# A kernel of linear attention and a gated feed-forward layer: own products of late blocks in halves of 64 keys, past products per head, in two phases over two PSUM banks

## The chip, the cores and the metric

One Trainium2 chip, one of its cores. The metric is the device time of one execution in microseconds, the median of three runs. A NeuronCore has a matrix engine (TensorE, PE in the profile, its weight loads PEld), a vector engine (DVE), a scalar engine (ACT), GpSimd (POOL), and SyncE (SP), which issues most DMAs here. Each works through its own list of instructions in order, and they wait for each other on semaphores. TensorE writes to PSUM, which has 8 banks of 2 KB in each of 128 partitions.

## The reference

`r`, `k`, `v`, `w` have the shape (4, 8, 768, 48): batch, heads, tokens, head dimension. Per head a 48 × 48 state runs over the tokens; its output goes through a feed-forward layer from 384 to 2048 and back.

```python
for t in range(S):
    kt, vt, rt, wt = (k[:, :, t], v[:, :, t], r[:, :, t], w[:, :, t])
    cur = np.einsum('bhd,bhe->bhde', u[None] * kt, vt)
    y[:, :, t] = np.einsum('bhd,bhde->bhe', rt, state + cur)
    state = wt[:, :, :, None] * state + np.einsum('bhd,bhe->bhde', kt, vt)
...
x = attn_out.transpose(0, 2, 1, 3).reshape(B * S, H * D)
h = x @ w_in
g = h * np.cos(h)
return g @ w_out
```

## The kernel before

**Chunks and blocks.** The tokens are cut in 24 chunks of 128 (six for each of four sequences). Two chunks make a block `i`, 12 blocks in all. Blocks 0 and 1 hold the first chunks of the four sequences, which have no past. A chunk holds eight heads as four pairs `p` with two heads `h` each; head `h` of a pair lies in partitions 64h to 64h + 47 (`rows(h)`).

**What a chunk needs.** VectorE makes products of the decays and scales `r` and `k` by them. `att_scores` makes k·r (`pa`); `placed` puts the allowed half of them into `asb`, on whose diagonal GpSimd has put the bonus terms (`picked`). `asb[h][:, p]` is a matrix of 128 keys by 128 queries of which the part above the diagonal counts. For chunks from 6 on (`ALL_OF`), the pairs 2 and 3 (`TURNED`) have the two halves of 64 keys and of 64 queries in swapped order, and `in_order` swaps the queries back as it reads. The output `y` of a chunk is the sum of two kinds of products:
- own products (`att_own`): `v` by `asb`, the keys of the chunk itself;
- past products (`att_past`): the state before the chunk (`past`) by the scaled `r`.

Both write to `py`, two banks of three groups of 128 columns for the two chunks of a block. The 48 output rows of a head lie as 32 rows in the group kt = 0 or 2 (`LONG`, eight places for a chunk) and 16 rows in the group kt = 1, where two heads share 32 rows (`middle`). Before the change an own product has 128 keys by 32 columns of `v` for 128 queries, 16 for a chunk; a past product has 48 rows for the places of `LONG` (L490) and 112 rows, both heads together, for the four middles (L486). `att_state` then makes the chunk's contribution to the state (`pst`, L423), in all blocks but the last two.

**The feed-forward layer.** ScalarE casts `py` to `xT` (`high`), VectorE makes the rest that the cast lost (`low`). A block has eight slots; `mm1` of a slot makes `ph` from `xT` and the weights (18 products of 256 columns, L571), `gate` runs over four engines (steps I, S, N, M, H, L), and `mm2`, two slots later, adds 12 products of 384 columns to `acc` (L589).

**The order.** It is written by hand: the string `START` for the slots of blocks 0 and 1, then for each slot a row of `PLAN`, whose tokens name a step and a chunk or block. A block's own products, past products and state sums are the tokens `o`, `p`, `s` in row 6 of the block before:

```python
"o+1 p+1 s+1 mm1 load+7 lv+6 lv+7 X+1 n+1 I S c+4 N M mm2 H L d+4",
```

For block 2 they stand near the end of `START` (`o2 L13 p2 mm2.12 mm2.13 I15 ... s2`). `load` and `lv` are DMAs of SP, `X` makes `xT`, `n` adds up the state, `c` ends with the next pick of `asb`, `d` places the next `past`. PSUM banks of the kind "a" are taken in turn by `bank`; from block 2 on there are four of them (`BANKS`, stage 3), used by `pa`, `pt`, `py` and `pst`.

Of the kernel before, what the change touches and what calls it, by code (L numbers as in the profile page):

```python
# [10 lines left out]
F32 = mybir.dt.float32  # L11
# [11 lines left out]
C = 128  # L23
HD = 48
NP = 4
R96 = 2 * HD
ROW = 64
# [3 lines left out]
BLK = 2  # L31
# [11 lines left out]
BANKS = dict(a=("a0", "a1", "a2", "acc0", "acc1"), h=("h0", "h1", "h2")), dict(a=("a0", "a1"), h=("h0", "h1")), dict(a=("a0", "a1", "a2"), h=("h0", "h1", "h2")), dict(a=("a0", "a1", "a2", "h2"), h=("h0", "h1"))  # L43
PAIR_W = 2 * HD + 16
VW = NP * PAIR_W
TURNED = 2
ALL_OF = 6
# [44 lines left out]
             o="a lv", s="t d lv", p="o d")  # L92
# [3 lines left out]
def rwkv_cos_ffn(ctx: ExitStack, tc: tile.TileContext, tr, tn, tv, u, ut, wts, w, rkw, vst, us, xs, out):  # L96
    nc = tc.nc
# [5 lines left out]
    FU = 512 // BT  # L103
    wts = wts.bitcast(I16)

    cst = ctx.enter_context(tc.tile_pool(name="cst", bufs=1))
# [3 lines left out]
    ps = fast.enter_context(tc.tile_pool(name="ps", bufs=1, space=bass.MemoryType.PSUM))  # L110
    turn = {"a": 0, "h": 0}
# [26 lines left out]
    wholes = cst.tile([R, NG, NP], F32, name="wholes")  # L138
    wmax = cst.tile([128, 1], F32, name="wmax")
    nc.vector.memset(wmax, 0.0)  # L140
    ones = cst.tile([128, 1], F32, name="ones")
    nc.vector.memset(ones, 1.0)
    past = [cst.tile([R, NP, R96], F32, name="past%d" % n) for n in range(BLK)]
# [293 lines left out]
    def v_col(p, h):  # L437

        return p * PAIR_W + h * (HD + 16)

    def att_own(i):

        py = [bank("a", [128, 3, C], "py") for half in range(2)]

        def at(kt, n, q):

            side, col = divmod(kt * BLK + n, 3)
            return py[side][32 * q:32 * q + 32, col]

        outs[i] = py, at  # L450
        for step, n in enumerate(sorted(range(BLK), key=lambda n: placed_at.get(i * BLK + n, n))):
            a = atts[i * BLK + n]

            def long_ones(sides, heads):
                for kt, p, h, q in LONG:
                    if kt in sides and h in heads:
                        col = v_col(p, h) + 16 * h
                        nc.tensor.matmul(out=at(kt, n, q), lhsT=a["v"][:, col:col + 32], rhs=in_order(a, a["asb", h][:, p], p),  # L458
                                         start=step == 0, stop=a["c"] == 0, skip_group_check=True)

            def middle(h):
                for p in range(NP):
                    col = p * PAIR_W + (48 if h else 32)
                    nc.tensor.matmul(out=at(1, n, p), lhsT=a["v"][:, col:col + 32], rhs=in_order(a, a["asb", h][:, p], p),  # L464
                                     start=False, stop=a["c"] == 0, skip_group_check=True)

            if step == 0:
                long_ones((0, 2), (0, 1))
                middle(0)
                middle(1)  # L470
            else:
                alone = 0 if n == BLK - 1 else 2
                long_ones((0, 2), (0,))
                middle(0)
                long_ones((alone,), (1,))
                long_ones((2 - alone,), (1,))
                middle(1)

    def att_past(i):

        py, at = outs.pop(i)
        two = [atts[i * BLK + n] for n in range(BLK)]
        if two[0]["c"] > 0:
            for n, a in enumerate(two):
                for p in range(NP):
                    nc.tensor.matmul(out=at(1, n, p), lhsT=a["past"][:, p, 32:64], rhs=in_order(a, a["r3"][:, p], p),  # L486
                                     start=False, stop=True, skip_group_check=True)
            for n, a in enumerate(two):
# [12 lines left out]
        def low(side):  # L501
            low_part("x", halves_of["x"][:, 1, side], py[side].rearrange("p k t -> p (k t)"), halves_of["x"][:, 0, side])

        def less(side):
            nc.tensor.matmul(out=py[side].rearrange("p k t -> p (k t)"), lhsT=nident, rhs=halves_of["x"][:, 0, side], start=False, stop=True, skip_group_check=True)

        def taken(side):
            nc.scalar.copy(out=halves_of["x"][:, 1, side], in_=py[side].rearrange("p k t -> p (k t)"))
# [50 lines left out]
    def mm1(t, half=None):  # L559
        i, u = seq[t]  # L560
        if not half:
            for j in range(BLK):
                att(i * BLK + j, "x")
            units[t] = bank("h", [C, FU, BT], "ph")
        xT, ph = xts[i], units[t]
        for fi in range(FU) if half is None else (half,):
            steps_of = [(kt, a, b) for kt in range(KT) for a, b in PASSES]
            if half is not None:
                steps_of.sort(key=lambda x: (x[1], x[2]))
            for n, (kt, a, b) in enumerate(steps_of):  # L570
# [240 lines left out]
    return [b * NCB + c for c in range(NCB) for b in range(n // NCB)]  # L811


def x_pieces():

    for kt, p, h, q in LONG:
        yield p, h, 16 * h, kt, 32 * q, 32
    for h in range(2):
        for p in range(NP):
            yield p, h, 0 if h else 32, 1, 32 * p + 16 * h, 16  # L820


def one_by_one(tc, rkw, vst, us, xs, out, ident, halves, wgt, gate):
# [147 lines left out]
```

## Time and profile before

| | |
|---|---|
| median of three runs | 507.66 us (507.04 to 508.62) |
| the profiled execution's own time | 509.25 us |
| its span, first to last instruction | 507.5 us |
| busy: PE, PEld | 501.5 us, 487.5 us |
| busy: DVE, ACT, POOL | 378.9, 256.0, 202.5 us |
| granted TensorE clock, mean | 0.992 of 2.4 GHz |

The page and the views behind it show one profiled execution. Busy is the time in which at least one instruction of an engine ran; products on TensorE overlap, so a row of a timeline gives the start of its first record and the time to the end of its last. "[0.20 <-X]" at a row's end is the idle time of the engine before it and what ended it. An fp32 product of the program stands as two records in the trace, an fp32r product (L571, L589) as one.

### The profile page before, as it was taken

What the parts mean: (1) busy time and instruction counts of PE and PEld (TensorE: products, weight loads), DVE (VectorE), ACT (ScalarE), POOL (GpSimd) and SP (SyncE); (2) the same over time, 40 slices, a digit from 0 to 9 for tenths busy, and PEclk for the clock granted to TensorE, in tenths of its full rate; (3) what the DMA queues carried; (4) which work ended last, traced back from release to release, by engine and by line L of the source; (5) the groups of instructions that cost most, each with busy time, mean ns of one, the idle gap of its engine ahead of it and who ended that gap; (6) DMA issues with size and microseconds to landing.
All of it is one profiled execution on the core that took longest, in us unless ns stands there. A gap on an engine that the chain in (4) does not pass through costs nothing.

```text
span 507.5 us, 12744 instructions
## 1 busy us (share of the span) xinstructions
PE 501.5 (99%) x5334; PEld 487.5 (96%) x5334; DVE 378.9 (75%) x669; ACT 256.0 (50%) x440; POOL 202.5 (40%) x273
## 2 busy tenths in 40 slices
PE   8999999999999999999999999999999999999997
PEld 8899999999999999999999999999999999999997
DVE  7989999777969758848947946956966975587633
ACT  2769788525355444444445435435444544544543
POOL 3434546435445335334333524523533533423330
PEclk9979999999999999999999999999999999999999
DMA  8978550142052051051040132113105103013001
GB/s 270 416 292 286 228 227 2 63 162 96 34 193 63 1 193 63 1 194 52 13 172 36 51 113 83 63 53 141 63 4 192 62 3 125 33 56 132 32 3 34
DMA packets 17324, 54.59 MB, mean 108 GB/s; under 512 B 2032, under 2 KB 8688, under 8 KB 17264
## 3 DMA queue, kind: packets, MB, share of 16 engines
q1 hardware_dynamic: 17120, 53.64, 29.7%
q8 instruction: 43, 0.70, 0.6%
q14 instruction: 17, 0.14, 0.1%
q10 hardware_dynamic: 144, 0.10, 0.1%
HBM read 49.02 MB, written 4.72 MB: 106 GB/s over the span
## 4 chain that ended last, share of the span: by engine, by line
PE 95%; DMA 2%; SPq 1%; ACT 0%; issue 0%; DVE 0%; DVEq 0%; ACTq 0%
PE ph L571 41%; PE acc L589 40%; PE pa L378 3%; DMA raw<-wts 2%; PE py L458 2%; PE py L464 2%; PE pst L423 2%; PE pt L401 2%; PE py L490 1%; PE py L486 1%; PE pa L370 1%; PE pc L307 1%; SPq L244 1%; SPq L262 0%; SPq L177 0%
## 5 line engine op out<-in xcount | busy, mean ns | idle before, releaser
L171 POOL TENSOR_TENSOR gs<-rr,gs 128x256 fp32r<-128x256 f32 x188 | 148.6, 811 | 236.9 <-ACT gs L168 214.2
L571 PE MATMUL ph<-xT,w 128*128 128x256 f32 x1728 | 222.2, 283 | 0.2 <-DVE w L202 0.2
L571 PEld LDWEIGHTS ph<-xT,w 128*128 128x128 f32 x1728 | 214.2, 190 | 2.3 <-PE py L490 0.4
L589 PE MATMUL acc<-w,gs 128*128 128x384 f32 x1152 | 215.6, 337 | 0.0
L589 PEld LDWEIGHTS acc<-w,gs 128*128 128x128 f32 x1152 | 196.1, 188 | 0.3 <-issue 0.2
L537 DVE SCALAR_TENSOR_TENSOR rr<-rr,ph 128x512 f32<-128x512 int32 x96 | 65.5, 682 | 63.6 <-ACT rr L534 62.5
L550 ACT ACTIVATE rr<-rr,quarter 128x512 f32<-128x512 f32 x96 | 69.5, 724 | 79.9 <-DVE rr L537 79.7
L534 ACT ACTIVATE rr<-ph 128x512 int32<-128x512 f32 x96 | 57.3, 597 | 68.3 <-PE ph L571 67.8
L168 ACT CAST gs<-rr 128x512 fp32r<-128x512 f32 x88 | 54.6, 621 | 63.2 <-DVE rr L551 39.1
L551 DVE TENSOR_TENSOR rr<-rr,ph 128x512 f32<-128x512 f32 x96 | 65.5, 682 | 22.3 <-ACT rr L550 20.0
L331 POOL TENSOR_SCALAR_AFFINE_SELECT asb<-cd 128x512 f32<-128x512 f32 x48 | 40.8, 876 | 53.2 <-DVE cd L321 35.5
L392 DVE COPY_PREDICATED asb<-turned_mask,pa 64x128 f32<-64x128 uint8 (+1 forms) x108 | 33.6, 346 | 2.1 <-POOL asb L331 0.3
L279 DVE TENSOR_TENSOR_SCAN ee<-tt,one_e 112x516 f32<-112x516 f32 (+1 forms) x25 | 31.6, 1269 | 2.0 <-DMA tt<-tr 2.0
L285 DVE TENSOR_TENSOR_SCAN tt<-tt,inj 112x516 f32<-112x516 f32 x24 | 30.3, 1262 | 0.8
L171 DVE TENSOR_TENSOR xT<-py,xT 128x384 fp32r<-128x384 f32 x22 | 11.3, 551 | 21.4 <-ACT xT L168 21.4
L192 ACT ACTIVATE top<-raw 128x768 f16<-128x768 bf16 x16 | 17.5, 1091 | 2.7 <-DMA raw<-wts 2.7
L458 PE MATMUL py<-asb,v 128*32 128x128 f32 x384 | 17.4, 276 | 0.0
L200 DVE CUSTOM_DVE_ANT_0 h<-h,top 128x1536 uint16<-128x1536 uint16 x16 | 16.1, 1005 | 1.7 <-ACT top L192 0.9
L464 PE MATMUL py<-asb,v 128*32 128x128 f32 x384 | 17.1, 273 | 0.0
L168 ACT CAST xT<-py 128x384 fp32r<-128x384 f32 x24 | 10.3, 482 | 12.7 <-PE py L490 11.6
L168 ACT COPY past<-dd 48x192 f32<-48x192 f32 x40 | 14.0, 349 | 2.7 <-DVE dd L354 2.4
L378 PEld LDWEIGHTS pa<-tt 48*64 48x64 f32 x576 | 12.9, 133 | 2.2 <-issue 2.2
(89 smaller groups left out, 364.4 us busy)
## 6 DMA issues: line engine op xcount, KB each, us to landing
tt<-tr SPq DMA_DIRECT2D x22, 770.5 KB, 6.6
raw<-wts SPq DMA_DIRECT2D x16, 767.8 KB, 6.9
rk<-tn SPq DMA_DIRECT2D x18, 384.0 KB, 3.2
v<-tv SPq DMA_DIRECT2D x24, 224.0 KB, 4.7
ww<-w SPq DMA_DIRECT2D x6, 768.0 KB, 5.1
out<-ob SPq DMA_DIRECT2D x23, 192.0 KB, 2.0
tt<-tr SPq DMA_DIRECT2D x4, 256.0 KB, 4.0
tt<-tr SPq DMA_DIRECT2D x1, 258.5 KB, 4.3
```

Of the source, the lines that this page charges most:

```text
L168: (nc.scalar.copy if E[name] is nc.scalar else E[name].tensor_copy)(out=out, in_=in_)
L171: E[name].tensor_tensor(out=out, in0=full, in1=high.bitcast(F32), op=ALU.subtract)
L279: nc.vector.tensor_tensor_scan(out=ee[:, pairs].rearrange("p a t -> p (a t)")[:, ::-1], data0=wp[:, cols][:, ::-1], data1=one_e[:, pairs]. ...
L285: nc.vector.tensor_tensor_scan(out=wp[:, 0:W129], data0=wp[:, 0:W129], data1=inj.rearrange("p a t -> p (a t)"), initial=0.0, op0=ALU.mult, ...
L331: nc.gpsimd.affine_select(out=asb, in_=col.unsqueeze(2).to_broadcast([C, NP, C]), pattern=[[0, 4], [1, C]], compare_op=ALU.is_equal, fill= ...
L392: nc.vector.copy_predicated(*(which(x) for x in (a["asb", h], turned_mask, pa[h])))
L534: nc.scalar.activation(made["rr"].bitcast(I32), ph, AF.Copy, scale=INV2PI / W_SCALE, bias=0.25)
L537: nc.vector.scalar_tensor_tensor(out=made["rr"], in0=made["rr"].bitcast(I32), scalar=-2.0 * math.pi * W_SCALE, in1=ph, op0=ALU.mult, op1=A ...
L550: N=lambda: nc.scalar.activation(made["rr"], made["rr"], AF.Sin, scale=1.0 / W_SCALE, bias=quarter),
L551: M=lambda: nc.vector.tensor_tensor(out=made["rr"], in0=made["rr"], in1=ph, op=ALU.mult), H=high, L=low)
L571: nc.tensor.matmul(out=ph[:, fi], lhsT=wgt[u * FU + fi][:, 0, a, kt * 128:(kt + 1) * 128], rhs=xT[:, b, kt], start=n == 0, stop=n == 3 * K ...
L589: nc.tensor.matmul(out=accs[i][j][:, :DM], lhsT=gs[:, a, fi, j * C:(j + 1) * C], rhs=wgt[u * FU + fi][:, 1, b], start=u == 0 and fi == 0 a ...
```

## The change

For blocks 3 to 11, `att_own` now only takes the two banks. `att_past` makes the products in two phases. Own products are cut in two halves of 64 keys each, of which the half that is earlier in time is multiplied for all 128 queries and the later one for its last 64 queries only (the quarter left out is masked). Past products are all 48 rows by 32 columns, the middles too, one for each head. In a phase the products in the lower 64 rows of the array write to one bank and those in the upper 64 rows to the other; the second phase swaps the banks. Between the phases stand a product of one column (`apart`) into a bank of its own, the state sums, and a second `apart`. Each bank of `py` now holds its three groups as kt = 0, 1, 2, and kt = 2 holds the other chunk: so `ph` reads `xT` for kt = 2 in two halves of 128 tokens in swapped order, and the casts write three pieces. The middles of the second heads move by two places (`middle_at`). In block 2 the own products stay at full height; the past products stand in two phases around them, and a ScalarE copy (`seen_past`) reads what the first phase wrote before the own products write there.

```diff
+    def apart(tag):
+
+        nc.tensor.matmul(out=ps.tile([C, 512], F32, tag=tag, name="apart")[:32, :1], lhsT=ident[:ROW, :32], rhs=ident[:ROW, :1], start=True, stop=True)
+
+    def past_products(i, at, phase, begins):
+
+        two = [atts[i * BLK + n] for n in range(BLK)]
+        ends = [(kt, phase ^ h ^ kt // 2, p, h, q, 64 * h) for kt, p, h, q in LONG]
+        middles = [(1, phase ^ h, p, h, middle_at(p, h), 32) for h in range(2) for p in range(NP)]
+        for kt, n, p, h, q, col in ends + middles:
+            a = two[n]
+            nc.tensor.matmul(out=at(kt, n, q), lhsT=a["past"][rows(h), p, col:col + 32], rhs=in_order(a, a["r3"][rows(h), p], p),
+                             start=begins and kt != 1, stop=True, skip_group_check=True)
+
+    def own_products(i, at, phase):
+
+        two = [atts[i * BLK + n] for n in range(BLK)]
+
+        def half(lower, kt, p, h, q, whole):
+            n = phase ^ lower ^ kt // 2
+            a = two[n]
+            keys = slice(ROW, C) if lower else slice(0, ROW)
+            col = p * PAIR_W + (48 if h else 32) if kt == 1 else v_col(p, h) + 16 * h
+            x = a["asb", h][keys, p]
+            out, x = (at(kt, n, q), in_order(a, x, p)) if whole else (at(kt, n, q)[:, ROW:], x[:, keys])
+            nc.tensor.matmul(out=out, lhsT=a["v"][keys, col:col + 32], rhs=x,
+                             start=phase == 0 and whole and kt != 1, stop=False, skip_group_check=True)
+
+        for places in LONG, [(1, p, h, middle_at(p, h)) for h in range(2) for p in range(NP)]:
+            for whole in (True, False):
+                for lower in range(2):
+                    for kt, p, h, q in places:
+                        if (lower == (p >= TURNED)) == whole:
+                            half(lower, kt, p, h, q, whole)
+
     def att_own(i):
...
-            side, col = divmod(kt * BLK + n, 3)
-            return py[side][32 * q:32 * q + 32, col]
+            return py[n ^ kt // 2][32 * q:32 * q + 32, kt]
 
         outs[i] = py, at
+        if i * BLK >= ALL_OF:
+            return
+        old = atts[i * BLK]["c"] > 0
+        if old:
+            past_products(i, at, 0, True)
+            nc.scalar.copy(out=seen_past, in_=at(1, 1, NP - 1)[:, :1])
...
+        if old:
+            past_products(i, at, 1, False)
 
     def att_past(i):
 
         py, at = outs.pop(i)
-        two = [atts[i * BLK + n] for n in range(BLK)]
-        if two[0]["c"] > 0:
-            for n, a in enumerate(two):
-                for p in range(NP):
-                    nc.tensor.matmul(out=at(1, n, p), lhsT=a["past"][:, p, 32:64], rhs=in_order(a, a["r3"][:, p], p),
-                                     start=False, stop=True, skip_group_check=True)
-            for n, a in enumerate(two):
-                for kt, p, h, q in LONG:
-                    nc.tensor.matmul(out=at(kt, n, q), lhsT=a["past"][rows(h), p, 64 * h:64 * h + 32],
-                                     rhs=in_order(a, a["r3"][rows(h), p], p), start=False, stop=True, skip_group_check=True)
+        if i * BLK >= ALL_OF:
+            for phase in range(2):
+                own_products(i, at, phase)
+                past_products(i, at, phase, False)
+                if phase == 0:
+                    turn["a"] += 1
+                    tag = BANKS[stage[0]]["a"][turn["a"] % len(BANKS[stage[0]]["a"])]
+                    apart(tag)
+                    att(i, "s")
+                    apart(tag)
...
-            halves_of["x"] = xts[i].rearrange("p o k t -> p o (k t)").rearrange("p o (s n) -> p o s n", s=2)
-            copy("xh", halves_of["x"][:, 0, side], py[side].rearrange("p k t -> p (k t)"))
+            halves_of["x"] = xts[i].rearrange("p o k (s t) -> p o s k t", s=2)
+            copy("xh", halves_of["x"][:, 0, side], py[side])
...
-                nc.tensor.matmul(out=ph[:, fi], lhsT=wgt[u * FU + fi][:, 0, a, kt * 128:(kt + 1) * 128], rhs=xT[:, b, kt],
+                tokens = xT[:, b, kt] if kt < 2 else xT[:, b, kt].rearrange("p (n t) -> p n t", n=BLK)[:, ::-1]
+                nc.tensor.matmul(out=ph[:, fi], lhsT=wgt[u * FU + fi][:, 0, a, kt * 128:(kt + 1) * 128], rhs=tokens,
...
+def middle_at(p, h):
+
+    return (p + NP // 2 * h) % NP
```

How the instructions stand, first for a late block (block 3) on TensorE. A row has the line, the operation, output and inputs, the output's size (partitions by columns) and how many such follow each other. Before, own products, past products and state sums in a row:

```order
L458 MATMUL py<-asb,v 32x128 x8
L464 MATMUL py<-asb,v 32x128 x8
L458 MATMUL py<-asb,v 32x128 x4
L464 MATMUL py<-asb,v 32x128 x4
L458 MATMUL py<-asb,v 32x128 x4
L464 MATMUL py<-asb,v 32x128 x4
L486 MATMUL py<-tt,past_89 32x128 x4
L486 MATMUL py<-tt,past_90 32x128 x4
L490 MATMUL py<-tt,past_89 32x128 x8
L490 MATMUL py<-tt,past_90 32x128 x8
L423 MATMUL pst<-v,kn 64x48
L423 MATMUL pst<-v,kn 48x48
```

The same place of the changed kernel, the first phase up to the state sums (L467 is `own_products`, L453 `past_products`, L444 `apart`, L424 `att_state`):

```order
L467 MATMUL py<-asb,v 32x128 x8
L467 MATMUL py<-asb,v 32x64 x8
L467 MATMUL py<-asb,v 32x128 x8
L467 MATMUL py<-asb,v 32x64 x8
L453 MATMUL py<-tt,past_90 32x128 x2
L453 MATMUL py<-tt,past_91 32x128 x4
L453 MATMUL py<-tt,past_90 32x128 x6
L453 MATMUL py<-tt,past_91 32x128 x4
L444 MATMUL apart<-ident 32x1
L424 MATMUL pst<-v,kn 64x48
L424 MATMUL pst<-v,kn 48x48
```

After 16 state sums a second `apart` and the second phase with the same counts follow, then `ph`; so the state sums now stand inside the products of `py`, and 56 products have become 96. In blocks 10 and 11, which have no state sums, the two `apart` stand next to each other.

The second place is block 2 on TensorE in the changed kernel, from the end of a slot's `ph` to the next `acc` (L499 and L505 are what L458 and L464 were):

```order
L614 MATMUL ph<-xT,w_1206 128x256 x9
L453 MATMUL py<-tt,past_90 32x128 x2
L453 MATMUL py<-tt,past_91 32x128 x4
L453 MATMUL py<-tt,past_90 32x128 x6
L453 MATMUL py<-tt,past_91 32x128 x4
L499 MATMUL py<-asb,v 32x128 x8
L505 MATMUL py<-asb,v 32x128 x8
```

Before, the own products stood directly behind that `ph`, and the past products behind them. The rest of the own products follows, and then the past products of the second phase. On ScalarE the copy that TensorE waits for between them stands here, ahead of the next slot's first step of the gate (L576):

```order
L592 ACTIVATE rr<-rr,quarter 128x512
L169 CAST gs<-rr 128x512
L576 ACTIVATE rr<-ph 128x512
L169 CAST gs<-rr 128x512
L491 COPY seen_past<-py 32x1
L576 ACTIVATE rr<-ph 128x512
L592 ACTIVATE rr<-rr,quarter 128x512 x2
```

That row L491 is the only one added on ScalarE; the other engines keep their order, but for SP, which from block 3 on issues the two `v` loads of a block ahead of both its `tt` loads instead of between them.

## Rows read from the trace of the kernel before

**Rows 1.** The page: the span, and TensorE's busy time, share and instructions.

```profile
span 507.5 us, 12744 instructions
PE 501.5 (99%) x5334; PEld 487.5 (96%) x5334; DVE 378.9 (75%) x669; ACT 256.0 (50%) x440; POOL 202.5 (40%) x273
```

**Rows 2.** The page: the chain that ended last, by engine.

```profile
PE 95%; DMA 2%; SPq 1%; ACT 0%; issue 0%; DVE 0%; DVEq 0%; ACTq 0%
```

**Rows 3.** Timeline of PE, one late block: start us, us, instructions.

```profile
175.98 0.65 PE L458 MATMUL py<-asb,v 128*32 128x128 f32 x16
176.44 0.62 PE L464 MATMUL py<-asb,v 128*32 128x128 f32 x16
...
177.75 0.62 PE L486 MATMUL py<-tt,past 112*32 112x128 f32 x16
178.30 0.67 PE L490 MATMUL py<-tt,past 48*32 48x128 f32 x32
178.90 1.13 PE L423 MATMUL pst<-v,kn 128*64 128x48 f32 x32
179.96 1.21 PE L571 MATMUL ph<-xT,w 128*128 128x256 f32 x8
```

**Rows 4.** Line L490 of the whole span: duration in ns, min/median/max.

```profile
L490 PE MATMUL py<-tt,past x320: 269/269/294, 102.0 to 457.2; 48*32 48x128 f32 x160
```

**Rows 5.** Waits: us in total, times, longest us.

```profile
PEld py L490 <- issue: 2.0, 10, 0.2
PEld pst L423 <- PE py L490: 1.4, 7, 0.2
```

**Rows 6.** Timeline of PE, the scores of a late block.

```profile
165.90 1.57 PE L378 MATMUL pa<-tt 48*64 48x128 f32 x64
167.40 0.38 PE L571 MATMUL ph<-xT,w 128*128 128x256 f32 x1
```

**Rows 7.** Timeline, block 10, first own products and next `ph`.

```profile
416.19 0.65 PE L458 MATMUL py<-asb,v 128*32 128x128 f32 x16
...
419.11 0.50 PE L571 MATMUL ph<-xT,w 128*128 128x256 f32 x2
```

**Rows 8.** Timeline of PE, block 2, first own products and next `acc`.

```profile
99.64 0.65 PE L458 MATMUL py<-asb,v 128*32 128x128 f32 x16
...
102.56 0.97 PE L589 MATMUL acc<-w,gs 128*128 128x384 f32 x4
```

**Rows 9.** Timeline of all engines after the block of group 3.

```profile
179.01 0.86 ACT L168 CAST xT<-py 128x384 fp32r<-128x384 f32 x2 [1.28 <-PE py L490]
...
182.36 0.60 ACT L534 ACTIVATE rr<-ph 128x512 int32<-128x512 f32 x1 [2.50 <-PE ph L571]
182.99 0.69 DVE L537 SCALAR_TENSOR_TENSOR rr<-rr,ph 128x512 f32<-128x512 int32 x1 [1.93 <-ACT rr L534]
183.60 0.54 DVE L321 TENSOR_REDUCE cd<-rk 128x8 f32<-128x384 f32 x1
...
184.28 1.22 POOL L331 TENSOR_SCALAR_AFFINE_SELECT asb<-cd 128x512 f32<-128x512 f32 x2 [5.06 <-DVE cd L321]
```

**Rows 10.** Line L168, a helper's copies, by tile: duration in ns, min/median/max.

```profile
L168 ACT CAST xT<-py x24: 472/480/488, 22.6 to 457.9; 128x384 fp32r<-128x384 f32 x24
...
L168 ACT COPY cd<-pc x6: 154/165/238, 10.2 to 58.0; 128x8 f32<-128x8 f32 x6
L168 ACT COPY kn<-pt x6: 478/482/488, 12.6 to 79.5; 128x384 f32<-128x384 f32 x6
```

**Rows 11.** Timeline of ACT near block 2.

```profile
96.83 0.61 ACT L168 CAST gs<-rr 128x512 fp32r<-128x512 f32 x1
99.74 0.60 ACT L534 ACTIVATE rr<-ph 128x512 int32<-128x512 f32 x1 [2.30 <-PE ph L571]
```

**Rows 12.** The chain in order of time: start us, us, what.

```profile
171.86 2.10 PE ph L571 x18
173.96 2.09 PE acc L589 x12
```

More of the change, by code (lines that the diff above doesn't have):

```diff
@@ L140, in rwkv_cos_ffn @@
     nc.vector.memset(wmax, 0.0)
+    seen_past = cst.tile([128, 1], F32, name="seen_past")[96:]
     ones = cst.tile([128, 1], F32, name="ones")
@@ L458, in long_ones @@
                         nc.tensor.matmul(out=at(kt, n, q), lhsT=a["v"][:, col:col + 32], rhs=in_order(a, a["asb", h][:, p], p),
-                                         start=step == 0, stop=a["c"] == 0, skip_group_check=True)
+                                         start=step == 0 and not old, stop=not old, skip_group_check=True)
             def middle(h):
@@ L463, in middle @@
                     col = p * PAIR_W + (48 if h else 32)
-                    nc.tensor.matmul(out=at(1, n, p), lhsT=a["v"][:, col:col + 32], rhs=in_order(a, a["asb", h][:, p], p),
-                                     start=False, stop=a["c"] == 0, skip_group_check=True)
+                    nc.tensor.matmul(out=at(1, n, middle_at(p, h)), lhsT=a["v"][:, col:col + 32], rhs=in_order(a, a["asb", h][:, p], p),
+                                     start=False, stop=not old, skip_group_check=True)
             if step == 0:
@@ L471, in att_own @@
             else:
-                alone = 0 if n == BLK - 1 else 2
                 long_ones((0, 2), (0,))
                 middle(0)
-                long_ones((alone,), (1,))
-                long_ones((2 - alone,), (1,))
+                long_ones((2,), (1,))
+                long_ones((0,), (1,))
                 middle(1)
+        if old:
+            past_products(i, at, 1, False)
     def att_past(i):
         py, at = outs.pop(i)
-        two = [atts[i * BLK + n] for n in range(BLK)]
-        if two[0]["c"] > 0:
-            for n, a in enumerate(two):
-                for p in range(NP):
-                    nc.tensor.matmul(out=at(1, n, p), lhsT=a["past"][:, p, 32:64], rhs=in_order(a, a["r3"][:, p], p),
-                                     start=False, stop=True, skip_group_check=True)
-            for n, a in enumerate(two):
-                for kt, p, h, q in LONG:
-                    nc.tensor.matmul(out=at(kt, n, q), lhsT=a["past"][rows(h), p, 64 * h:64 * h + 32],
-                                     rhs=in_order(a, a["r3"][rows(h), p], p), start=False, stop=True, skip_group_check=True)
+        if i * BLK >= ALL_OF:
[8 more added lines that the diff above has]
+                    apart(tag)
         halves_of = {}
@@ L497, in high @@
                 xts[i] = buf("xT", [128, 2, KT, BT], F32R)
-            halves_of["x"] = xts[i].rearrange("p o k t -> p o (k t)").rearrange("p o (s n) -> p o s n", s=2)
-            copy("xh", halves_of["x"][:, 0, side], py[side].rearrange("p k t -> p (k t)"))
+            halves_of["x"] = xts[i].rearrange("p o k (s t) -> p o s k t", s=2)
+            copy("xh", halves_of["x"][:, 0, side], py[side])
         def low(side):
-            low_part("x", halves_of["x"][:, 1, side], py[side].rearrange("p k t -> p (k t)"), halves_of["x"][:, 0, side])
+            low_part("x", halves_of["x"][:, 1, side], py[side], halves_of["x"][:, 0, side])
         def less(side):
-            nc.tensor.matmul(out=py[side].rearrange("p k t -> p (k t)"), lhsT=nident, rhs=halves_of["x"][:, 0, side], start=False, stop=True, skip_group_check=True)
+            nc.tensor.matmul(out=py[side], lhsT=nident, rhs=halves_of["x"][:, 0, side], start=False, stop=True, skip_group_check=True)
         def taken(side):
-            nc.scalar.copy(out=halves_of["x"][:, 1, side], in_=py[side].rearrange("p k t -> p (k t)"))
+            nc.scalar.copy(out=halves_of["x"][:, 1, side], in_=py[side])
         for side in range(2):
@@ L819, in x_pieces @@
         for p in range(NP):
-            yield p, h, 0 if h else 32, 1, 32 * p + 16 * h, 16
+            yield p, h, 0 if h else 32, 1, 32 * middle_at(p, h) + 16 * h, 16
 def one_by_one(tc, rkw, vst, us, xs, out, ident, halves, wgt, gate):
```

## Prediction

> **What bounds the kernel now.** I read the page first: TensorE (PE) is busy for 501.5 of 507.5 us [rows 1]. The chain that ended last is PE for 95% of the span [rows 2], so a microsecond taken out of PE's stream is a microsecond of the kernel, as long as no other engine becomes late. Then I read PE's own timeline over one block of the steady part. The stretch that the change rewrites runs from the first own product at 175.98 to the first `ph` product at 179.96, that is 3.98 us [rows 3]; in between stand the own products (L458, L464), the past products (L486, L490) and the state sums (L423). Each fp32 matmul of the program leaves two records (a block's 32 own products show as 64 records: the two rows of 16 shown and four of 8), and I count records below.
>
> Four prices come from this stretch.
> - **Four tiles at once, 128 columns.** From L464's start at 176.44 to L486's at 177.75 lie 48 records in 1.31 us: 27.3 ns each, 0.109 us for four [rows 3].
> - **Eight tiles at once, 128 columns.** L490 is the only line with 48 rows by 32 columns. Its 32 records cover 0.67 us from first start to last end, and one lasts 0.269 [rows 3, 4], so 31 steps took 0.40 us: 12.9 ns each. That is eight in the 0.109 us that four take above.
> - **A change of tile shape.** L490's loads stand idle 0.2 us before the first, in 10 blocks, and L423's 0.2 us after it, in 7 [rows 5]. Counted as starts: L490 to L423 is 0.60 us for four eights (0.436), so a shape's stretch costs its groups plus about 0.16. The own stretch agrees: 175.98 to 178.30 is 2.32 for 80 records (2.18), 0.14 more.
> - **64 columns.** The scores (L378) run 32 records of 128 and 32 of 64 columns, four at once, in 1.50 us from start to start [rows 6]. Less eight fours at 0.109 (0.87) and 0.16 for the shape, 0.47 is left for eight fours of 64 columns: 0.058 each.
>
> **The change part by part.** *Late blocks with a state sum (seven: blocks 3 to 9).* Before, 3.98 us. After, a phase has 32 own records of 128 columns, 32 of 64 and 32 past records of 128, eight tiles at once: 4 × 0.109 + 4 × 0.058 + 4 × 0.109 = 1.10, and 0.16 for the shape, 1.26. The two `apart` products have one column; nearest is a record that must wait for its tile, so I take 0.03 for the first and 0.06 for the second, which follows a change of shape with an unhidden load; the bounds are 0 and 0.2 each (the wait of [rows 5]). The state sums stay at 1.06 (178.90 to 179.96). Sum: 1.26 + 0.03 + 1.06 + 0.06 + 1.26 = 3.67, a gain of 0.31 a block, 2.2 us in seven. The products alone go from 2.62 (80 records in fours, 32 in eights) to 2.20; the second stretch of 64-row shape and the two `apart` take 0.11 of that back. For a one-column product the Trainium skill (TensorEngine Tiling (Array Packing), "Instruction Overhead") says that it lasts as long as one of 60 columns. By that, as an estimate, each `apart` would be two records of 0.025 us, 0.05, and the sum 0.1 us nearer to zero; no row here has such a product between tiles.
>
> *The last two blocks (10, 11)* have no state sum. Before, 416.19 to 419.11 is 2.92 us [rows 7]. After, two phases without a change of shape between: 2 × 1.10 + 0.16 + 0.06 = 2.42; but the second `apart` now follows the first directly and waits for its completion, for which I take the 0.2 to 0.3 of a change of shape [rows 5]. Gain 0.2 each, 0.4 us (0.5 at most).
>
> *Block 2* is rewritten the other way: past products of phase 0, a copy on ScalarE that reads them, own products at full height, past products of phase 1. Before, 99.64 to 102.56 is 2.92 us [rows 8]. After: past 0.436, its last record ends about 0.2 later, at 100.3; ScalarE starts some 0.05 after (L490 ends at 178.97, the cast starts at 179.01 [rows 3, 9]), the copy takes 0.165 like the small copy of `cd` [rows 10], and PE starts at about 100.6. Own products 1.75 + 0.14, past 0.436 + 0.16: `acc` at 103.1, 0.55 us later. PE's queue stands behind that wait, and everything on PE with it. ScalarE must be free for it: its record at 99.74 comes after the copy in the new order, and it ran nothing else from then on that precedes it [rows 11]. If it had to finish one 0.6 us action first, the loss would be 1.15.
>
> *Covered edits.* `py` is complete about 0.65 us later in a late block, because phase 1 comes after the state sums. The casts to `xT` and their low parts move with it; ScalarE then stands idle 2.50 us before its next action and VectorE 1.93 us [rows 9], so it costs nothing; without that cover it would be 0.65 a block on the gate, not on PE. GpSimd's next pick of `asb` waits for VectorE's `cd` at 183.6, 5.06 us idle [rows 9], later than the end of phase 1. SP now issues `v` before both `tt` loads, each about 1 us later; the data are first read a block later. The bank that `apart` takes was unused from the state sum to the next transposes. The casts write three pieces of 128 instead of 384 in a row: `kn`, which reads 48 pieces apart, takes ScalarE 482 ns and the cast 480 [rows 10], so nothing.
>
> *The right operand of `ph` for kt = 2* is read as two halves in swapped order, in a third of 1728 matmuls, 576. A `ph` record costs 2.10/18 = 0.1167 us and an `acc` record of 384 columns 2.09/12 = 0.1742 [rows 12]; the difference prices 128 columns at 0.0575, so 256 columns are 0.115 and what is fixed in a record is 0.0017. Half of the own records already read swapped halves and stand in the same 27.3 ns. I take nothing; the bound is one more fixed part, 576 × 0.0017 = 1.0 us.
>
> **Sum.** −2.2 − 0.4 + 0.55 = −2.05 us. The profiled execution took 509.25 us (span 507.5 and 1.75 around it), 1.6 over the median of 507.66; the change lies inside the span, so I take it from the median: **505.6 us**, 0.4% faster. What the measurement can tell from no change is about 0.3%, 1.5 us.
>
> **Rivals.**
> - **The 64-column eights don't go faster than the 128-column ones.** Nothing in the trace starts records closer than 12.9 ns over a run; 0.058 for eight asks for 7.3 ns, each with its own weight load. If starts hold at 13.6 ns (0.109 for eight), a phase costs 0.20 more, 18 phases 3.7 us: 509.3, slower. It decides from 0.114 more a phase (2.05/18), that is 0.086 us for such an eight. Against it: L490's loads and products were started in 0.40 us together, 64 starts, so the gap is not one of the array's.
> - **Long runs can't be fed.** L490's 32 records stand behind an idle of 0.2 us in which a queue could fill. The longest denser run is L378's, 64 in 1.34 us, 21 ns each. At that pace 96 records take 2.0 us instead of 1.10: 18 × 0.9 = 16 us more, 522 at the far end, and 511 where a full queue covers most. The Trainium skill (TensorE: Matmul & The Clock Gate, "Wait — 56ns, not 53.3ns?") says that starts never come closer than about 25 ns however few the columns. By that figure, as an estimate, a phase would be 2.4 us and the kernel near 529. L490's 12.9 ns is under it, so across tiles the rule doesn't hold at least for 32 records.
> - **The waits around `apart` are real.** `apart` and the state sum carry waits on PE's own semaphore. If each costs the 0.2 us of L423's wait once more, two in seven blocks, it is 2.8 us: 508.4, no measurable change. Against it: the counts are those of the bank's earlier users, long reached.
> - **The swapped halves or block 2's copy cost their upper bound.** +1.0 or +0.6: 506.2 to 506.6, at the edge of no change.
>
> **Chances.** Forecast 0.58 (its own range 504.9 to 506.3); 64-column eights no faster 0.17; long runs not fed 0.04; waits real 0.10; upper bounds of small terms 0.08; more gain than forecast, shape changes hidden by the queue (0.1 less at each, 504.7), 0.03. Faster: most of the forecast and the last, 0.53. No change: the forecast's rest, the waits, the small terms and the mild end of the first rival, 0.28. Slower 0.19. The range goes from 504.8, a little under the forecast's own, to 509.4, which takes in the first rival.
>
> **What would show it.** The stretch of a late block, first own product to first `ph`, should measure 3.67 us; eights of 64 columns at 0.058; the two phases alike, 1.10 and 0.16; the last two blocks' stretches at 2.7; block 2's at 3.5 with one PE idle of 0.3 before its own products that ends with ScalarE's copy. `ph` should stay at 2.10 for 18. The forecast is wrong if a phase measures over 1.2, if PE waits for its own semaphore for over 0.1, or if an idle of PE on another engine appears where there is none now.

## The result, and the profile after

The changed kernel takes 514.18 us (median of five runs, 511.59 to 514.76), the kernel before 507.56 (507.04 to 508.62): a ratio of 1.0119 [1.0091, 1.0147], slower. The forecast was 505.6, its range 504.8 to 509.4. It was wrong, and in its sign.

First the page of the kernel after: the span, TensorE's busy time, the queue that brings instructions (packets, MB, share), and the chain that ended last by engine. Under it the same queue's row of the kernel before, which was not shown above.

```profile
span 512.4 us, 14276 instructions
...
PE 503.1 (98%) x6106; PEld 487.1 (95%) x6106; DVE 379.1 (74%) x669; ACT 256.3 (50%) x441; POOL 204.2 (40%) x273
...
q8 instruction: 49, 0.80, 0.6%
...
PE 94%; DMA 2%; SPq 1%; issue 1%; ACT 0%; DVE 0%; DVEq 0%; ACTq 0%
```

```profile
q8 instruction: 43, 0.70, 0.6%
```

PE is still the chain. It has 772 product records and as many loads more than before [rows 1]; six more packets of 16 KB bring them (0.80 MB in 49 now); and 1% of the chain is now "issue", waiting for nothing that the profile shows, where it was 0% [rows 2]. TensorE's granted clock doesn't account for the loss: it is 0.996 of 2.4 GHz in this execution.

The timeline of PE over the second late block, which answers to [rows 3]:

```profile
176.43 0.94 PE L467 MATMUL py<-asb,v 64*32 64x128 f32 x53
...
177.26 0.63 PE L453 MATMUL py<-tt,past 48*32 48x128 f32 x24
...
177.93 1.13 PE L424 MATMUL pst<-v,kn 128*64 128x48 f32 x32
179.00 0.19 PE L444 MATMUL apart<-ident 64*32 64x1 f32 x1
179.01 0.33 PE L467 MATMUL py<-asb,v 64*32 64x128 f32 x6
...
180.56 0.62 PE L614 MATMUL ph<-xT,w 128*128 128x256 f32 x3
```

From 176.43 to 180.56 are 4.13 us, where [rows 3] had 3.98 and the forecast 3.67. Phase 0 with its change of shape and the first `apart` is 1.50 (to 177.93), forecast as 1.29; the sums and the second `apart` are 1.08, forecast as 1.12; phase 1 is 1.55 (from 179.01), forecast as 1.26. So even an undisturbed late block loses 0.16.

Of the seven late blocks with a state sum only three are undisturbed. The first one, PE's timeline in phase 1:

```profile
137.41 0.19 PE L444 MATMUL apart<-ident 64*32 64x1 f32 x1
137.43 0.33 PE L467 MATMUL py<-asb,v 64*32 64x128 f32 x6
137.47 0.17 PE L444 MATMUL apart<-ident 64*32 64x1 f32 x1
137.47 0.90 PE L467 MATMUL py<-asb,v 64*32 64x128 f32 x36
139.20 0.42 PE L467 MATMUL py<-asb,v 64*32 64x128 f32 x16 [0.84 <-issue]
...
140.20 0.39 PE L614 MATMUL ph<-xT,w 128*128 128x256 f32 x1
```

In the middle of a run of the same line, whose data have long been there, PE stands idle for 0.84 us; the block's stretch takes 5.35 (134.85 to 140.20). Such gaps stand in blocks 3, 6, 7 and 8; their stretches are 5.35, 4.68, 5.01 and 5.29 against 4.14 in blocks 4, 5 and 9. The waits (us in total, times, longest) show the gaps as "issue", and one wait more:

```profile
PEld py L467 <- issue: 5.2, 12, 1.1
...
PE py L467 <- issue: 2.1, 3, 0.8
...
PEld apart L444 <- PE py L453: 0.8, 2, 0.4
```

The second `apart` of blocks 10 and 11 waits 0.4; the profile puts the wait down to the past products (L453) ahead of the first `apart`, and whether it is them or the first `apart` isn't shown. The stretch is 3.28 where [rows 7] had 2.92. Block 2, PE's timeline and a row of its loads, answers to [rows 8]:

```profile
98.37 0.67 PE L453 MATMUL py<-tt,past 48*32 48x128 f32 x32
98.97 0.81 PE L499 MATMUL py<-asb,v 128*32 128x128 f32 x16
...
101.61 0.97 PE L632 MATMUL acc<-w,gs 128*128 128x384 f32 x4
```

```profile
99.35 0.16 PEld L499 LDWEIGHTS py<-asb,v 128*32 128x32 f32 x8 [0.23 <-ACT seen_past L491]
```

That is 3.24 against 2.92. The sum of the stretches: 7 × 0.16 = 1.1, gaps 1.21 + 0.54 + 0.87 + 1.15 = 3.8, 0.7 in the last two blocks, 0.3 in block 2, together 5.9 of the 6.6 us between the medians. Between the two profiled executions it is 4.9, since this one reached block 2 1.3 us earlier (98.37 against 99.64 in [rows 8]).

### The profile page after: what moved, and what is told of

Read it like the earlier page. It is cut to its first block, busy times and chain, and to the rows that moved or that the text cites. A ratio compares the mean times of both kernels' runs of the same rounds, so it can differ in the third digit from the quotient of the medians.

```text
span 512.4 us, 14276 instructions
## 1 busy us (share of the span) xinstructions
PE 503.1 (98%) x6106; PEld 487.1 (95%) x6106; DVE 379.1 (74%) x669; ACT 256.3 (50%) x441; POOL 204.2 (40%) x273
## 4 chain that ended last, share of the span: by engine, by line
PE 94%; DMA 2%; SPq 1%; issue 1%; ACT 0%; DVE 0%; DVEq 0%; ACTq 0%
PE ph L614 40%; PE acc L632 39%; PE py L467 3%; PE pa L379 3%; PE py L453 2%; DMA raw<-wts 2%; PE pst L424 2%; PE pt L402 1%; PE pa L371 1%; PE pc L308 1%; SPq L245 1%; SPq L263 0%; PE py L499 0%; PE py L505 0%; PE apart L444 0%
## 5 line engine op out<-in xcount | busy, mean ns | idle before, releaser
L576 ACT ACTIVATE rr<-ph 128x512 int32<-128x512 f32 x96 | 57.4, 597 | 59.7 <-PE ph L614 59.1
L169 ACT CAST xT<-py 128x384 fp32r<-128x384 f32 x24 | 10.3, 483 | 24.6 <-PE py L453 23.5
L467 PE MATMUL py<-asb,v 64*32 64x128 f32 (+1 forms) x1152 | 20.4, 248 | 2.1 <-issue 2.1
L467 PEld LDWEIGHTS py<-asb,v 64*32 64x32 f32 x1152 | 16.7, 105 | 5.2 <-issue 5.2
L453 PE MATMUL py<-tt,past 48*32 48x128 f32 x640 | 17.1, 275 | 0.2 <-issue 0.2
```

What stands on the lines that cost most here:

```text
L467: nc.tensor.matmul(out=out, lhsT=a["v"][keys, col:col + 32], rhs=x, start=phase == 0 and whole and kt != 1, stop=False, skip_group_check=True)
L576: nc.scalar.activation(made["rr"].bitcast(I32), ph, AF.Copy, scale=INV2PI / W_SCALE, bias=0.25)
```

## Experiments

Two questions: why a phase takes 1.5 instead of 1.26, and what the gaps are. *Supply theory*: behind the first 32 records of a run, records on eight tiles come only at a limited pace; its rival is the array or the banks. *Fetch theory* for the gaps: instructions come in packets of 256, and the dense stretch uses one up before the next is there; its rivals are the transfers or waits of the block. All kernels are edits of the changed one. Gaps are what a block's stretch has over the undisturbed one.

| kernel | us | ratio to before | undisturbed late block, us | gaps, us |
|---|---|---|---|---|
| changed | 514.18 | 1.0119 [1.0091, 1.0147] | 4.14 | 3.8 in 4 blocks |
| full_halves | 517.9, one run | | 4.25 | 5.0 in 5 |
| no_halves | 502.7, one run | | 3.35 | none |
| halves_first | 511.16 | 1.0072 [1.0046, 1.0098] | 3.94 | 3.0 in 3 |
| ph_between | 512.04 | 1.0089 [1.0059, 1.0119] | 4.14, two parts | 0.85 in 1, in `ph` |
| shifted | 517.05, one run | | 4.14 | 6.6 in 6 |
| own_in_fours | 510.97 | 1.0059 [1.0041, 1.0078] | 4.16 | none |
| both_remedies | 510.21 | 1.0044 [1.0027, 1.0060] | 3.93, two parts | none |

**full_halves.**

```diff
-            out, x = (at(kt, n, q), in_order(a, x, p)) if whole else (at(kt, n, q)[:, ROW:], x[:, keys])
+            out, x = at(kt, n, q), in_order(a, x, p)
```

> The changed kernel, but the 64-column products of the own part take all 128 columns (the added quarter of asb holds zeros), so the number and order of PE's instructions stay the same. Array theory (records of a phase cost what their columns cost, and the lost time lies elsewhere): four groups of eight in a phase go from 0.058 to 0.109 us, +0.20 a phase, an undisturbed late block from 4.14 to 4.55 us. Supply theory (from the 33rd record of a phase on, records come no closer than about 13.6 ns, whatever their columns): only the two groups among a phase's first 32 records get dearer, +0.10 a phase, 4.34 us a block. Instruction-fetch theory for the long stalls: the instructions are as many, so the same four late blocks (the 1st, 4th, 5th and 6th) show PE gaps of 0.4 to 1.1 us, unless the longer phase covers a part.

Block 5's stretch on PE's timeline:

```profile
219.49 1.17 PE L467 MATMUL py<-asb,v 64*32 64x128 f32 x64
...
223.75 0.39 PE L614 MATMUL ph<-xT,w 128*128 128x256 f32 x1
```

Doubling the columns of a third of the records adds 0.06 a phase (4.25), under both expectations and much nearer to supply (0.10) than to array (0.20): the 64-column records had bought almost nothing. The four blocks have their gaps again, behind the same record (174 in block 3, as above), and block 4 has one too. The number of instructions is the same, only the time differs; block 4, with the same instructions, had no gap in the changed kernel, so their number alone doesn't decide whether one comes.

**no_halves.**

```diff
-            for whole in (True, False):
+            for whole in (True,):
```

> The changed kernel without the own products of 64 columns: it leaves that part of the computation out (the later 64 queries of a block miss a half of their keys). A phase has 32 own and 32 past records of 128 columns. Array theory: four groups of 0.058 less, 0.23 a phase, an undisturbed late block from 4.14 to about 3.68 us. Supply theory: 32 records less at about 13.6 ns, 0.4 to 0.45 a phase, about 3.3 us. Fetch theory: a block's stretch has 128 loads and products fewer, and the stalls of 0.4 to 1.1 us shrink to under 0.5 us in sum; if the stalls come from the transfers of tt and v that are issued in the stretch, they stay in the same blocks.

Block 4's stretch on PE's timeline:

```profile
173.90 0.67 PE L467 MATMUL py<-asb,v 64*32 64x128 f32 x32
174.36 0.69 PE L453 MATMUL py<-tt,past 48*32 48x128 f32 x32
...
177.25 0.39 PE L614 MATMUL ph<-xT,w 128*128 128x256 f32 x1
```

3.35: 0.39 a phase for 32 records whose columns are worth 0.23. What they cost is 12 ns each, near what supply says (13.6 ns, 0.4 to 0.45 a phase). All gaps are gone, though the transfers are issued where they were.

**halves_first.**

```diff
-        for places in LONG, [(1, p, h, middle_at(p, h)) for h in range(2) for p in range(NP)]:
-            for whole in (True, False):
+        for whole in (False, True):
+            for places in LONG, [(1, p, h, middle_at(p, h)) for h in range(2) for p in range(NP)]:
...
-                             start=phase == 0 and whole and kt != 1, stop=False, skip_group_check=True)
+                             start=phase == 0 and not whole and kt != 1, stop=False, skip_group_check=True)
```

> The changed kernel with all 32 records of 64 columns at the head of each phase, then the 32 own and 32 past ones of 128 columns. Supply theory: the first 32 records run at the array's pace, so the short ones cost 0.23 us there, and the 64 behind them 13.6 ns each and a hiccup of 0.08; a phase with its shape goes from 1.50 to about 1.35, an undisturbed late block from 4.14 to about 3.85, the kernel 2 to 3 us below the changed one (511 to 512 where it is 514.2). Array theory: the order makes no difference, 4.14.

The same records in another order take 3.94 instead of 4.14 (175.33 to 179.27 in block 4), where 3.85 was expected: 0.20 of the 0.47 that lay between the block and the forecast's 3.67. To the array alone the order would make no difference. In nine blocks that is 1.8 of the 3.0 us in the median; 0.8 is the gap fewer.

**ph_between.**

```diff
                     att(i, "s")
+                    up(0)
+                    early.append(i)
                     apart(tag)
...
             if e == "mm1":
-                up(0)
+                if early:
+                    early.pop()
+                else:
+                    up(0)
```

> The changed kernel with the slot's 18 ph products (2.1 us) moved from behind phase 1 to between the state sums and phase 1. Nothing is added, and the transfers are issued at the same place. Fetch theory (a block's stretch uses up instructions faster than they are fetched): the gaps of 0.4 to 1.1 us in four late blocks vanish, 3.4 us, and the second apart of the last two blocks no longer waits for the first, 0.4 us: about 510.4. Transfer theory (the loads of tt and v disturb PE): the gaps stay, about 513.8. Both: the two phases themselves stay at 1.50 and 1.45.

PE's timeline in block 3, and later in block 8:

```profile
134.21 0.94 PE L467 MATMUL py<-asb,v 64*32 64x128 f32 x53
...
136.78 2.37 PE L616 MATMUL ph<-xT,w 128*128 128x256 f32 x18
139.08 0.19 PE L444 MATMUL apart<-ident 64*32 64x1 f32 x1
...
140.65 2.36 PE L634 MATMUL acc<-w,gs 128*128 128x384 f32 x12
142.84 2.26 PE L616 MATMUL ph<-xT,w 128*128 128x256 f32 x18
...
340.77 1.80 PE L616 MATMUL ph<-xT,w 128*128 128x256 f32 x14 [0.68 <-issue]
```

The gaps in the products are gone with the same instructions in another order; one is left behind the fourth `ph` of block 8. To see what the order costs, the `ph` and `acc` behind the block have to be counted in. The same in an undisturbed block (5) of the changed kernel:

```profile
216.75 0.94 PE L467 MATMUL py<-asb,v 64*32 64x128 f32 x53
...
220.89 2.39 PE L614 MATMUL ph<-xT,w 128*128 128x256 f32 x18
223.12 2.25 PE L632 MATMUL acc<-w,gs 128*128 128x384 f32 x12
225.21 0.98 PE L614 MATMUL ph<-xT,w 128*128 128x256 f32 x7
```

From the first own product to the next slot's `ph` are 8.63 us, against 8.46 there: `ph` takes 2.30 instead of 2.23, `acc` 2.19 instead of 2.09. Between full height and small tiles PE now changes once more, at 0.17 a block, 1.2 us in the seven blocks with state sums; in the last two it eats up what the vanished wait of `apart` gave back. That and the gap that stayed (0.85) more than account for the 1.6 us by which my 510.4 was short.

**rates.** Behind the kernel's last products:

```diff
+        def bench(name, cols, groups, pause):
+            two = [ps.tile([C, 512], F32, tag=x, name=name) for x in ("h0", "h1")]
+            for n in range(groups * 8):
+                h, q = n // 4 % 2, n % 4
+                nc.tensor.matmul(out=two[h][32 * q:32 * q + 32, :cols], lhsT=ident[ROW * h:ROW * h + ROW, :32],
+                                 rhs=ident[ROW * h:ROW * h + ROW, :cols], start=True, stop=True)
+            rest = ps.tile([C, 512], F32, tag="a0", name="rest")[:, :C]
+            for n in range(pause):
+                nc.tensor.matmul(out=rest, lhsT=ident, rhs=ident, start=True, stop=True)
```

> The changed kernel, and behind its last acc product, before the votes are read, runs of 96 records on eight tiles of 64 rows by 32 columns (constants, no waits in a run, no transfers of inputs going on): 128, 64, 32 and 1 columns, each run twice, with 16 products of 128 by 128 between runs to let the queue fill; last a run of 640 records of 128 columns with no rest. Array theory: starts go with the columns, 13.6 ns a record at 128, 7 at 64 and below, over the whole run. Supply theory in the form of a fixed number of instructions under way (32 loads and 32 products, each pair held for its own load and run time): the first 32 records at the array's pace, from the 33rd on 13.6 ns at 128 columns, about 11 at 64, 10.5 at 32 and 9.7 at 1. Supply theory in the form of a fixed rate at which instructions come: 13.6 ns from the 33rd on at all four widths. Fetch theory: the run of 640 records uses 1280 instructions at 256 a packet, so PE stops in it about every 128 records, for what a fetch takes over the 1.75 us that 128 records last, 0.5 to 1.2 us each; transfer theory: no stop. The body is that of the changed kernel, and its late blocks should show gaps in the same blocks at the same record as there.

PE's timeline, the first run of each width (the second repeats it) and the long run:

```profile
512.20 1.59 PE L846 MATMUL r_whole<-ident 64*32 64x128 f32 x96
...
517.49 1.17 PE L846 MATMUL r_half<-ident 64*32 64x64 f32 x96
...
522.36 1.02 PE L846 MATMUL r_quarter<-ident 64*32 64x32 f32 x96
...
527.08 0.97 PE L846 MATMUL r_one<-ident 64*32 64x1 f32 x96
...
551.30 2.62 PE L846 MATMUL r_long<-ident 64*32 64x128 f32 x168
555.08 2.03 PE L846 MATMUL r_long<-ident 64*32 64x128 f32 x128 [1.17 <-issue]
558.54 2.03 PE L846 MATMUL r_long<-ident 64*32 64x128 f32 x128 [1.43 <-issue]
562.55 2.03 PE L846 MATMUL r_long<-ident 64*32 64x128 f32 x128 [1.98 <-issue]
566.28 1.53 PE L846 MATMUL r_long<-ident 64*32 64x128 f32 x88 [1.70 <-issue]
```

And the same view of windows that end with the 32nd record of a run:

```profile
512.20 0.67 PE L846 MATMUL r_whole<-ident 64*32 64x128 f32 x32
...
517.49 0.45 PE L846 MATMUL r_half<-ident 64*32 64x64 f32 x32
...
522.36 0.36 PE L846 MATMUL r_quarter<-ident 64*32 64x32 f32 x32
...
527.08 0.33 PE L846 MATMUL r_one<-ident 64*32 64x1 f32 x32
```

A record lasts 269, 216, 193 and 167 ns at the four widths (the tile view's medians); without the last one's duration the first 32 of 64 columns take 0.234 us, 31 steps of 7.5 ns, or 0.060 for eight, close to the 0.058 of the forecast. The 64 behind them take 0.95 − 0.23 = 0.72, 11.2 each. For 128, 32 and 1 columns the later ones come to 14.4, 10.3 and 10.0. So it is neither the array (7 or less) nor one fixed rate (13.6).

The figures expected of 32 pairs under way (13.6, 11, 10.5, 9.7) are within 1 ns, but the single starts in the trace don't bear that form out. At 128 columns they keep 0.109 for eight over the whole run (the 14.4 comes from where the count cuts an eight); at the other widths a step of some 0.07 to 0.09 stands about the 32nd record, and from the 41st on they go at 9.5 ns (64 columns), 8.3 (32) and 8.3 (1), the last two alike though their records last 193 and 167. What sets the pace behind the step stays open.

The changed kernel's own starts (phase 0 of block 4) show the same: the two eights of 64 columns among the first 32 records take 0.056 and 0.055; then comes a step of 0.08; the two such eights behind it take 0.079 and 0.073; and three eights of 128 columns near them take 0.124 to 0.132 instead of 0.109, which rates, with one width in each run, doesn't explain.

For the gaps, the long run, with no transfer of inputs beside it and no waits, stops behind its 168th product record and then behind every 128, that is 256 instructions with their loads, for 1.2 to 2.0 us. The same shows in the kernel itself: from block 2 on, the traces of all these runs hold 27 idles of PE of 0.2 us or more, and by the number of PE's loads, products and semaphore instructions ahead of them all 27 stand at the same remainder of 256, to within one instruction. Each stop inside a late block is at the second packet's end of its stretch; a stretch with a single one never stops.

**shifted.**

```diff
+            for again in range(16 if j == 19 else 0):
+                nc.tensor.matmul(out=filled[:32, :1], lhsT=ident[:ROW, :32], rhs=ident[:ROW, :1], start=True, stop=True)
```

> The changed kernel with 16 products of one column more at the very start, which are 64 loads and products. Fetch theory: PE stops where a packet of instructions ends, so in each late block that had a gap the place of the gap moves to 64 loads and products (32 products' records) earlier in the stretch: the 1st late block's from behind the 174th product record to the 142nd, the 4th's from the 203rd to the 171st, the 5th's from the 170th to the 138th, the 6th's from the 137th to the 105th; how long each lasts may change, and one may come or go. Theory of a wait or transfer of the block itself: the gaps stay at the same records. Time 511 to 516 either way.

Phase 1 of block 3 on PE's timeline, against the same place of the changed kernel above:

```profile
136.02 0.19 PE L444 MATMUL apart<-ident 64*32 64x1 f32 x1
136.03 0.31 PE L467 MATMUL py<-asb,v 64*32 64x128 f32 x4
136.07 0.17 PE L444 MATMUL apart<-ident 64*32 64x1 f32 x1
136.10 0.38 PE L467 MATMUL py<-asb,v 64*32 64x128 f32 x6
137.03 0.84 PE L467 MATMUL py<-asb,v 64*32 64x128 f32 x48 [0.54 <-issue]
```

The gap comes behind 10 own records of the phase instead of 42: exactly the 32 product records that were added at the start of the program. In block 6 it moves from 203 to 171 as well. Blocks 7 and 8 lost theirs, and 5, 9, 10 and 11 got one. Where a stop can stand is decided by where a packet ends; whether it comes is not decided by that alone, since packets end at the expected places of blocks 7 and 8 too. This one run, with 64 instructions of padding, is 2.9 us over the changed kernel's median, 2.8 of it in the gaps.

**own_in_fours.**

```diff
     def own_products(i, at, phase):
 
         two = [atts[i * BLK + n] for n in range(BLK)]
+        for n in range(0 if phase else BLK):
+            a = two[n]
+            for kt, p, h, q in LONG + [(1, p, h, middle_at(p, h)) for h in range(2) for p in range(NP)]:
+                col = p * PAIR_W + (48 if h else 32) if kt == 1 else v_col(p, h) + 16 * h
+                nc.tensor.matmul(out=at(kt, n, q), lhsT=a["v"][:, col:col + 32], rhs=in_order(a, a["asb", h][:, p], p),
+                                 start=n == 0 and kt != 1, stop=False, skip_group_check=True)
+        return
```

> The changed kernel with the halves undone: in the late blocks the own products take all 128 keys in one, four tiles at once as before the change, all in front of phase 0's past products; past per head in 48 rows, two banks, the phases and the apart products stay. Runs of eights are then 32 records long. Supply theory: own 64 records at 27.3 ns and 0.14, each past run 0.44 and 0.16, state sums 1.06, apart 0.05: 4.0 us an undisturbed late block, where the changed kernel has 4.14 and the kernel before 3.98. Fetch theory: a block's stretch holds a quarter fewer instructions, and no stall over 0.2 us is left: the kernel at 507.5 to 509. If the stalls come from the order or the banks and not from the number of instructions, they stay, and the time is over 511.

Block 4's stretch on PE's timeline:

```profile
175.43 1.95 PE L463 MATMUL py<-asb,v 128*32 128x128 f32 x64
...
179.59 0.38 PE L621 MATMUL ph<-xT,w 128*128 128x256 f32 x1
```

4.16, no gaps. The 4.0 that I wrote was a slip: its terms are 1.89 + 0.60 + 0.60 + 1.06 + 0.05 = 4.20. So past per head in two phases gains nothing by itself: 16 records of 112 rows at 27.3 ns (0.44) become 32 at 12.9 (0.41), and the second stretch of that shape costs its 0.16. The time is not within the 507.5 to 509 expected: blocks 3 to 9 give 1.3, the last two 0.8, block 2 0.3, of the 3.1 us over before; 0.7 lies outside them. What stands ahead of block 2 differs by as much between the profiled executions: block 2 starts anywhere from 96.95 (shifted) to 99.86 us (full_halves).

**both_remedies.** halves_first and ph_between together.

> The changed kernel with both remedies: the 64-column records first in each phase, and the slot's ph products between the state sums and phase 1. If the two losses are separate and add up: an undisturbed late block has 3.94 + 2.10 us with its ph where the order alone gives it, plus the 0.2 of the two changes of shape more around ph, 6.2 us, against 6.08 in the kernel before; seven such blocks +0.9, the last two +0.1 each, block 2 +0.32, and what is left of fetch gaps 0 to 0.9: 1.3 to 2.3 us over the kernel before, 509 to 510 us. If one remedy undoes the other (the fetch gaps come back, or the order stops helping), 511 or more. Below 507 would say that the sum of the stretches leaves something out.

2.53 us over before, a little above the expected 1.3 to 2.3. There is no gap in any block, and the two parts of a late block take 2.48 and 1.45, with 2.30 for `ph` between: 6.23, against 6.19 before, where the `ph` behind the state sums takes 2.20 and not 2.10; the `acc` behind phase 1 takes 2.19 to 2.22 instead of 2.09. That is 0.16 a block, 1.4 in nine, and with block 2 1.8 of the 2.53; the rest lies outside them. With both answered the change still doesn't pay. No version was found that beats the kernel before.

## Why the prediction was wrong

- **The step that failed** is "a phase has 32 own records of 128 columns, 32 of 64 and 32 past records of 128, eight tiles at once: 4 × 0.109 + 4 × 0.058 + 4 × 0.109 = 1.10". The term 4 × 0.058 is what was mis-sized: its price came from four tiles at once, and on eight it holds for the first 32 records of a run (0.060 in rates, 0.055 in the kernel). Behind those stand a step of about 0.08, the other 64-column eights at 0.073 to 0.079, and eights of 128 columns beside them at up to 0.132, so phase 0 is 1.50, 0.21 over its forecast with `apart`. The price of 128 columns alone holds: no_halves and rates have 0.109 for eight. Why the eights of 128 columns beside short ones are slower, some 0.06 of it, was not tested. The first rival, starts that hold at 13.6 ns, had the size (+0.20 a phase) and a chance of 0.17, but not the reason, since short records do start closer than that. "L490's loads and products were started in 0.40 us together" was taken against it; a run of exactly 32 could not show it.
- **The gaps** were not in the sum. "Long runs can't be fed" had the outcome, 511 to 522, and 0.04. Its queue that fills in an idle and then runs short is nearest to what a phase shows, but it priced that at 21 ns a record; that the time fell into its range is luck, since 3.8 us of it are the gaps. It counted queues of PE, not the packets that fill them. On the page stood 43 packets for PE's 5334 products and as many loads, some 250 each; a late block now issues 456 loads and products in 4.1 us instead of 288 in 4.0. At 27.3 ns a record, 128 records with their loads last 3.5 us; at 13.7, 1.75; the long run shows a packet every 3.5 to 4.0. The Trainium skill (Runtime: NRT & Kernel Launch, "Instruction fetch mechanics") has the same 256 instructions a block and says that fetching is mostly hidden, since instructions are dispatched more slowly than they are fetched. Here the second half doesn't hold: with eight tiles two instructions go in 13.7 ns, and stops of up to 2.0 us show.
- **`apart`.** In blocks with a state sum the two cost next to nothing, as forecast; the rival with real waits fell there. In the last two blocks the second waits 0.4, over the 0.2 to 0.3 taken.
- **Block 2** cost 0.32 instead of 0.55: the first four own products write to the bank that the copy doesn't read, and start at 98.97, before it; only the fifth waits for the copy, 0.23 us.
- **Swapped halves of `ph`.** Away from the rewritten stretch the chain has `ph` x18 at 2.10 as in [rows 12]: nothing, as forecast. The covered edits stayed covered; no other engine became the bound.

## What to carry to other kernels

A price read from a run of 32 short records need not hold for the 33rd: before making a run longer or denser, ask what supplies it behind that. Count instructions as a resource: cutting products in smaller pieces for more tiles at once doubles loads and products for the same array time, and where a stretch uses up 256 of them faster than a packet arrives, PE can stop, at places that move with every instruction added anywhere ahead. Work with few instructions per microsecond between two dense stretches hid the fetch in all blocks but one of ph_between, at the price of its changes of shape.

## What the runs showed of the hardware

- Start to start on eight tiles, from 1 to 128 columns: 5 to 13 ns for the first 32 records; from the 41st on 8.3 ns (1 and 32 columns), 9.5 (64) and 13.65 (128). The Trainium skill (TensorE: Matmul & The Clock Gate, "Wait — 56ns, not 53.3ns?") has about 25 ns as the least; across tiles these rows go well below it. The 32 records are 64 instructions with their loads, and the Trainium skill's table at the top of that page has 64 for the depth of the engine's queue; that the step comes from it was not tested apart.
- A stop for instructions costs 0.5 to 2.0 us, and where it can fall is set by the program alone; whether it comes and how long it lasts differs from run to run (block 6: 0.54 in the changed kernel, 0.99 in rates, which has the same body; block 4: none in either, 1.3 in full_halves, which has the same instructions). What in the fetch varies stays open.
- One more change between full height and small tiles costs PE about 0.17 us: 8.63 us from a late block's first own product to the next slot's `ph` in ph_between, 8.46 in the changed kernel.
